# Two ways to turn and spread memory probabilities in a recurrent attention kernel, and where twenty tail units stand

## The chip, the core and the metric

The kernel runs on one core of a Trainium2 chip. A core has five engines that work side by side: TensorE (PE, with its weight loads as PEld), VectorE (DVE), ScalarE (ACT), GpSimd (POOL) and SyncE (SP, which here issues most DMAs). The metric is device time in microseconds of one execution; lower is better. Line numbers with an L are those of the kernel before, unless the text says that they are of the changed kernel.

## What is computed

A layer norm, an attention with a recurrent memory over 64 segments, a second layer norm, and a feed-forward layer with squared relu, with two residual sums:

```python
h = x + A(layernorm(x)); out = h + B(layernorm(h))
# A: S = 2048 rows of Dm = 640, H = 32 heads of Dh = 128, M = 8 memory rows, segments of 32 rows
mem = mem0
for s in range(n_seg):
    h = jnp.concatenate([mem, xs], axis=1)            # 8 memory rows, 32 rows of the segment
    q, k, v = (einsum('btd,dhe->bhte', h, W) for W in (Wq, Wk, Wv))
    p = softmax(where(mask, q @ k.T * Dh ** -0.5, -1e9))  # a memory row sees all, a row only earlier ones
    o = einsum('bhte,hed->btd', p @ v, Wo)
    mem = o[:, :M]; outs.append(o[:, M:])
```

The memory rows of one segment's output are input of the next. This makes a chain of 64 steps that cannot be done side by side.

## The kernel before

**Segments.** Each call of `step(b, sp)` (L462) is one segment, s = 4b + sp. Its projections run over 32 rows: the 8 memory rows, and the first 24 rows of the segment. The last 8 rows of each segment ("tails") have their projections made in advance, four segments to a block of 32 rows: 16 blocks, four to a group. A group's tail rows are loaded with `load_tail_rows` (L125), normalised (`ln_stats`, `ln_norm`), transposed (`ln_transpose`, L197) and kept in `hTt`. Groups 0 to 2 are transposed on PE at the start of the kernel; group 3 (blocks 12 to 15) is loaded by four DMAs in segment 3 and transposed by a DMA in segment 6.

**Fill.** The tail projections are cut into units of four matmuls of 512 columns (`tail_units`, L324), and the wo projection of a finished block's tails into ten units of four or eight matmuls (`wo_tail_units`, L368). A plan (L901 to L931) holds them with a due segment and a segment from which they can run; `portion(s)` takes some for each segment, up to 8.05 per segment on average and nine at most, none in segment 0. They go to `fill`, and `run(fill, n)` issues them in PE's stream between the segment's own work. Values of a block's tails go to DRAM (`vt_d`) and come back as `vt4`.

**One segment on PE**, in the order of its stream: q (L562 on), k, q, k projections of two halves of the heads; scores of the memory rows for the first half of the heads (`scores(0)`, L505); v projection in pieces; scores of the segment's rows (`token_scores`, L601); `scores(1)`; the rest of v; some fill; values of the memory rows for the first half (`values(0)`, L551 and L556); more fill; the first 16 matmuls of the output projection wo (L270); `values(1)`; the other 48 of wo; the rest of the fill; values of the rows of the segment before (`token_values`, L426 and L431). Then o is summed out of PSUM (`wo_out`, L285 to L287) and turned into the next segment's hT (`mem_to_hT`, L387), for which the next q projection waits.

**Memory softmax.** For each half n of the heads, `soft1(n)` takes the maximum on DVE (L511) and the exponential on ACT (L516). `soft2(n)` takes the reciprocal of the sum (L522) and writes the four copies of the tail probabilities (L523). The probabilities lie as 128 rows (four groups g of 32) by 64 columns. The values matmul wants them turned, 32 x 32 by 32 x 32, and spread over a tile `pB` of 128 x (4 x 64) that is zero outside block (g, g). The two halves do this in different ways:

- Half 0 scales to 64 columns (L527), turns them (L538, `soft3`), and copies the four blocks into a `pB[0]` that was zeroed at the start (L541): one block by ACT, two by POOL, one by DVE, the last behind the maximum of half 1 (`then` of `soft1`).
- Half 1 multiplies with `own` while it scales (L530, 256 columns; `own` is 1 for the row's own group and 0 elsewhere, read with a broadcast), and turns all 256 columns (L533).

**Segment 0** has its projections done beforehand, in `start()` (L813), while the weights arrive: wv, wq, wk and then wo in eight pieces, all on SP's queue. `stream("q", ...)` and `stream("k", ...)` (L837) issue five pieces of the main projection each, with units of blocks 3 to 9 between them; five units are left over for segment 0. `SEG0` (L764) says how many units stand ahead of each quarter of wo in segment 0: none.

Of the kernel before, what the change touches and what calls it, by code (L numbers as in the profile page):

```python
# [9 lines left out]
ALU = mybir.AluOpType  # L10
# [6 lines left out]
def kernel(  # L17
# [16 lines left out]
    nc = tc.nc  # L34
# [90 lines left out]
    def load_tail_rows(g, eng=nc.sync):  # L125

        xt = s2.tile([128, D], BF16, tag="xt", name="xt")
        if g > 2:
            for b in range(4):
                eng.dma_start(out=xt[32 * b:32 * b + 32, :],  # L130
                              in_=x2d.rearrange("(b s t) d -> b t s d", s=4, t=SEG)[4 * g + b, HD:SEG, :, :])
        else:
            eng.dma_start(out=xt[:], in_=x2d.rearrange("(s t) d -> s t d", t=SEG)[16 * g:16 * g + 16, HD:SEG, :])
        xts["t", g] = xt

    o_ring = [const.tile([128, DQ], BF16, name="o%d" % k) for k in range(5)]
# [60 lines left out]
    def ln_transpose(b):  # L197

        xn = xns.pop(b)
        if not isinstance(b, tuple) and b > 0:  # L200
            nc.sync.dma_start(out=rows_in(b), in_=xn[:], transpose=True)
            return
        if isinstance(b, tuple) and b[1] > 2:
            hTt = s2.tile([128, DC, 4, TL, 4], BF16, tag="hTt", name="hTt", bufs=4)
            nc.sync.dma_start(out=hTt[:].rearrange("p c b k s -> p c (b k s)"), in_=xn[:], transpose=True)
            hTts[b[1]] = hTt
            return
        pt = mm.tile([128, 1024], BF16, tag="mm", name="pt")
        for c in range(DC):
            nc.tensor.transpose(out=pt[:, c * 128:(c + 1) * 128], in_=xn[:, c * 128:(c + 1) * 128], identity=ident[:])  # L210

        def out():
            if isinstance(b, tuple):
                hTt = s2.tile([128, DC, 4, TL, 4], BF16, tag="hTt", name="hTt", bufs=4)
                for dve, a0, a1 in ((False, 0, 12), (True, 12, 20)):
                    evac(dve, hTt[:].rearrange("p c b k s -> p (c b) s k")[:, a0:a1],
                         pt[:, 0:640].rearrange("p (a s k) -> p a s k", s=4, k=TL)[:, a0:a1])
                hTts[b[1]] = hTt
                return
            ptv = pt[:, 0:640].rearrange("p (c s t) -> p c s t", c=DC, s=4)  # L220
            nc.scalar.copy(out=rows_in(b).rearrange("p c (s t) -> p c s t", s=4)[:, :, :, 0:HD], in_=ptv[:, :, :, 0:HD])
        return out
# [239 lines left out]
    def step(b, sp, v=None):  # L462
# [43 lines left out]
                                     start=(j == 0), stop=(j == 3), skip_group_check=True)  # L506
            sms[n] = sm

        def soft1(n, then=None):
            mx = s2.tile([128, 1], F32, tag="mx", name="mx")  # L510
            nc.vector.tensor_reduce(out=mx[:], in_=sms[n][:, 0:NK], op=ALU.max, axis=AX.X, negate=True)  # L511
            if then:
                then()
            em = s2.tile([128, SEG + NK], BF16, tag="em", name="em", bufs=1)
            zm = s2.tile([128, 1], F32, tag="zm", name="zm")
            nc.scalar.activation(out=em[:, SEG:], in_=sms[n][:, 0:NK], func=ACT.Exp, bias=mx[:, 0:1], scale=1.0,  # L516
                                 accum_out=zm[:])
            ems[n], zms[n] = em, zm

        def soft2(n):  # L520
            rm = s2.tile([128, 1], F32, tag="rm", name="rm")
            nc.vector.reciprocal(out=rm[:], in_=zms[n][:])  # L522
            nc.vector.tensor_tensor(out=ems[n][:, 0:SEG].rearrange("p (j k) -> p j k", k=TL),  # L523
                                    in0=ems[n][:, 2 * SEG:].unsqueeze(1).to_broadcast([128, 4, TL]), in1=same[:], op=ALU.mult)
            if n == 0:
                pm = s1.tile([128, HG, TL], BF16, tag="pkt", name="pm")[:].rearrange("p i k -> p (i k)")
                nc.vector.tensor_scalar(out=pm, in0=ems[n][:, 0:2 * SEG], scalar1=rm[:, 0:1], scalar2=None, op0=ALU.mult)  # L527
                return pm
            pm = s1.tile([128, HG, 32], BF16, tag="pk", name="pm")[:].rearrange("p (g a) k -> p g (a k)", g=G)
            nc.vector.scalar_tensor_tensor(out=pm, in0=ems[n][:, 0:2 * SEG].unsqueeze(1).to_broadcast([128, G, 2 * SEG]),  # L530
                                           scalar=rm[:, 0:1], in1=own[:].unsqueeze(2).to_broadcast([128, G, 2 * SEG]),
                                           op0=ALU.mult, op1=ALU.mult)
            nc.vector.transpose(out=pBs[1][:], in_=pm)  # L533
            return pBs[1]

        def soft3(pm):
            pT = s1.tile([128, 2, 32], BF16, tag="pTt", name="pT")[:].rearrange("p u k -> p (u k)")
            nc.vector.transpose(out=pT, in_=pm)  # L538
            def part(g):
                r = slice(32 * g, 32 * g + 32)  # L540
                (nc.vector.tensor_copy, nc.scalar.copy, nc.gpsimd.tensor_copy, nc.gpsimd.tensor_copy)[g](out=pBs[0][r, g], in_=pT[r])  # L541
            for g in range(1, G):
                part(g)
            return pBs[0], lambda: part(0)

        def values(n, pB, po):
            cols = po[:, 0, 0:128]
# [49 lines left out]
        def token_scores(n):  # L597
            skv = view()
            for j in range(4):
                for g in range(G):  # L600
                    nc.tensor.matmul(skv[32 * g:32 * g + 32, n * 4 + j, :], lhsT=qT[:, n * 16 + g * 4 + j, :],  # L601
                                     rhs=kT[:, n * 16 + g * 4 + j, :], start=True, stop=True,
                                     skip_group_check=True)

        token_scores(0)
        if not ready:
            proj(wv, "half", lhs, 0, ps0, 2, DC)
# [2 lines left out]
            proj(wv, "half", lhs, 1, ps1, 0, 1)  # L610
        if not last:
            pm0 = soft2(0)
            pT0, then = soft3(pm0)
            scores(1)
            soft1(1, then)
        if not ready:
            proj(wv, "half", lhs, 1, ps1, 1, 2)
        token_scores(1)
# [4 lines left out]
            if last:  # L623
                nc.scalar.copy(out=v[:, 768:1024], in_=ps1[:, 256:512])
        if not last:
            pT1 = soft2(1)
        def causal(skv):
            nc.vector.tensor_tensor(out=skv[:, :, M:NK], in0=skv[:, :, M:NK],
                                    in1=mask[:].unsqueeze(1).to_broadcast([128, HG, SEG]), op=ALU.add)

        held = []
        if ready:
            run(fill, 10)
            run_late(0, 100)
        skv = view()
        po = po_tiles()
        if last:
            run(fill, 2, held, True)
            token_values(s - 1, *prevs[-2], po)
            token_out(s - 1, po)  # L640
            settle(held, True)
            run(fill, 100, held)
            settle(held, True)
            causal(skv)
        else:
            ahead = 0 if ready else (len(fill) + 1) // 2
            left = len(fill) - ahead
            run(fill, (ahead - 1) // 2, held, True)
            values(0, pT0, po[1][0])
            values_out(0, po[1][0])  # L650
            if not ready:
                nc.scalar.copy(out=v[:, 768:1024], in_=ps1[:, 256:512])
            run(fill, len(fill) - left, held)
            pw = chn.tile([128, 512], F32, tag="ch", name="pw")
            if not ready:
                wo_rounds(lambda p: oT[:, p, M:NK], pw, range(4))
            values(1, pT1, po[1][1])
            causal(skv)
            values_out(1, po[1][1])
            settle(held, True)  # L660
# [23 lines left out]
        if not last:  # L684
            if ready:
                for k in range(4):
                    run(fill, SEG0[k])
                    wo_rounds(lambda p: oT[:, p, M:NK], pw, [2 * k + h for h in (0, 1, 8, 9)])
            else:
                wo_rounds(lambda p: oT[:, p, M:NK], pw, range(4, 16))  # L690
# [70 lines left out]
    parked += [(hnT0[:, c, :], True) for c in range(DC)] + [(ht0[k][:, 0:512], True) for k in range(NK4)]  # L761
    parked += [(t, True) for t, _ in halves(oTts[1][:].rearrange("p h r -> p (h r)"))]
    writes = []
    SEG0 = (0, 0, 0, 0)  # L764
    hnTs = [hnT0[:], ck(DC * NT).rearrange("p (c t) -> p c t", c=DC)]
    ots = [ck(D) for _ in range(4)]
    fxs = [ck(D) for _ in range(4)]
# [45 lines left out]
    def start():  # L813
# [45 lines left out]
        for n in range(2):  # L859
            spread(n)  # L860
        tails_v_in(0, nc.gpsimd, 0, 1)
        run(units, 10)
        parked.append((s1.tile([128, D], BF16, tag="xn", name="parkx")[:, 0:512], False))
        units += [u for b in (8, 9) for u in tail_units(b, "v")] + tail_units(1, "q")
        stream("k", wk, kT)
        units += tail_units(1, "k")
        run(units, DC)
        fill.extend(units)
# [10 lines left out]
    load_tail_rows(2)  # L879
    load_w(wv, A_Wv, 4, 5)  # L880
    load_w(wq, A_Wq)
    load_w(wk, A_Wk)
    load_wo()
    ln_transpose(("t", 0))()
    ln_stats(("t", 1))
# [5 lines left out]
    nc.gpsimd.memset(mask[0:TL], 0.0)  # L891
    nc.gpsimd.affine_select(out=mask[0:TL], in_=mask[0:TL], compare_op=ALU.is_ge, fill=NEG, base=HD,
                            pattern=[[-1, SEG]], channel_multiplier=1)
    nc.gpsimd.memset(pBs[0][:], 0.0)
    nc.gpsimd.memset(own[:], 0.0)
    for g in range(G):
        nc.gpsimd.memset(own[32 * g:32 * g + 32, g:g + 1], 1.0)
# [7 lines left out]
            plan += [(4 * b - 3 + (which == "k"), 4 * b - 5, u[DC * n:DC * n + DC]) for n in range(2)]  # L905
    for b in range(10, NB):
        u = tail_units(b, "v")
        plan += [(b - 8 if b < 12 else 28 + 4 * (2 * b - 24 + n), 1 if b < 12 else 7, u[DC * n:DC * n + DC]) for n in range(2)]
    for b in range(NB - 1):
        plan.append(({NB - 4: NS - 3, NB - 2: NS - 1}.get(b, min(4 * b + 8, NS - 3)), 4 * b + 5, wo_tail_units(b)))  # L910
    plan.sort(key=lambda p: p[0])
    begun, paced = [], [0]

    def portion(s):
        n = {NS - 3: 482, NS - 2: 486}.get(s, round(8.05 * s)) - paced[0]
        got = []
        while True:
            if not begun:
# [3 lines left out]
                plan.remove(ready[0])  # L922
                begun.append(ready[0])
            d, _, u = begun[0]
            if len(got) >= min(n, 9) and d > s:
                break
            got.append(u.pop(0))
            if not u:
# [4 lines left out]
    for b in range(NB):  # L933
        for sp in range(4):
# [16 lines left out]
                nook += ln_parts(b + 2)  # L951
            if 0 < b < NB - 1 and sp == 1:
                ln_transpose(b + 1)
            if (b, sp) == (0, 3):
                load_tail_rows(3)
            if (b, sp) == (1, 0):
                late.insert(0, (1.15, lambda: ln_stats(("t", 3)), 4))
            if (b, sp) == (1, 1):
                mid.append(lambda: ln_norm(("t", 3)))
            if (b, sp) == (1, 2):  # L960
                ln_transpose(("t", 3))
            e = b * 4 + sp - (NS - 7)
            if (b, sp) == (1, 0):
                ffn_biases()
# [138 lines left out]
```

## Time and profile before

| what | us |
|---|---|
| median of three runs | 946.59 |
| the three runs | 945.86, 946.59, 948.37 |
| the profiled execution | 946.84 |
| its span, first to last instruction | 945.0 |
| start to the first segment's scores | about 50 |
| segments 1 to 62, each | 11.74 to 13.90 |

The profiled execution's span is 1.8 us shorter than its time. The mean granted clock of TensorE is 0.998 of full speed. PE executes 24760 matmuls. A timeline line reads: start, length (both in us), engine, source line, operation, output <- inputs, shape, count; a bracket gives the idle time of that engine before it and what ended it. A line of the windows view reads: stretch, length, and then busy time and number of instructions of PE, PEld, DVE, ACT and POOL, granted clock, share of the DMA engines, and GB/s. A line of the chain view in order of time reads: start, length, what.

### The profile page before, as it was taken

The page shows a single profiled execution, that of the slowest core. Times are in us where ns is not written, and L with a number is a line of the kernel's source. Part 1 is how long each engine was busy: PE and PEld are TensorE (multiplying, and loading weights), DVE is VectorE, ACT ScalarE, POOL GpSimd, SP SyncE. Part 2 cuts the span into 40 slices and gives each one's busy share as a digit, 9 for nine tenths or more (in the row PEclk, how much of TensorE's full clock was granted, in tenths as well). Part 3 has the DMA queues.
Part 4 walks back from the last instruction along what each step waited for, and adds up shares of the span by engine and source line. Part 5 has one row for each costly group of instructions (what it writes and reads, how often), then busy time and mean ns, then how long its engine had stood idle before and what let it go on. Part 6 is the DMA issues. An engine that isn't in the chain of part 4 may idle for free.

```text
span 945.0 us, 56036 instructions
## 1 busy us (share of the span) xinstructions
PE 918.3 (97%) x24760; PEld 524.0 (55%) x24760; DVE 681.4 (72%) x2068; ACT 571.7 (60%) x1586; POOL 309.7 (33%) x1003
## 2 busy tenths in 40 slices
PE   5979999999999999999999999999999999999998
PEld 2435555655565555555555555565555555565555
DVE  5167887777777777877787787777777788556632
ACT  2446666666666666766676666666666666523321
POOL 2023333333333333333333333333333344344300
PEclk9999999999999999999999999999999999999999
DMA  9982201020102001110101010101010221733320
GB/s 359 408 263 67 45 14 34 9 35 9 22 20 26 19 15 25 20 21 14 32 17 29 9 32 15 32 12 33 15 32 13 53 44 22 233 82 91 91 56 28
DMA packets 65779, 56.66 MB, mean 60 GB/s; under 512 B 37288, under 2 KB 61616, under 8 KB 63616
## 3 DMA queue, kind: packets, MB, share of 16 engines
q1 hardware_dynamic: 65392, 52.74, 20.1%
q8 instruction: 194, 3.18, 1.4%
q14 instruction: 49, 0.40, 0.1%
q0 software_dynamic: 128, 0.33, 0.1%
q10 hardware_dynamic: 16, 0.01, 0.0%
HBM read 38.37 MB, written 9.44 MB: 51 GB/s over the span
## 4 chain that ended last, share of the span: by engine, by line
PE 91%; DMA 4%; SPq 2%; DVE 1%; issue 1%; ACT 1%; DVEq 0%
PE ps L234 23%; PE px L234 21%; PE pw L270 15%; PE pk L234 7%; PE y L1060 6%; PE ps L1008 6%; PE ps L270 3%; PE po L551 2%; DMA wq<-in_A_Wq_dram 2%; PE po L426 2%; SPq L151 2%; PE ps L601 1%; PE sm L505 1%; DMA wo<-in_A_Wo_dram 1%; DMA wv<-in_A_Wv_dram 1%; PE po L556 1%
## 5 line engine op out<-in xcount | busy, mean ns | idle before, releaser
L234 PEld LDWEIGHTS <-hT 128*32 128x32 bf16 x7680 | 180.4, 96 | 160.4 <-DVE hT L387 20.4
L270 PE MATMUL pw<-wo,oT 128*32 128x320 bf16 x4224 | 168.8, 299 | 2.5 <-DMA wo<-in_A_Wo_dram 2.3
L234 PE MATMUL px<-wv,hT 128*32 128x512 bf16 x2520 | 166.0, 377 | 0.0
L270 PEld LDWEIGHTS <-oT 128*32 128x32 bf16 x4224 | 107.7, 96 | 41.6 <-ACT oT L246 19.6
L258 DVE STREAM_TRANSPOSE qT<-row 128x512 bf16<-128x512 bf16 x128 | 89.2, 697 | 36.1 <-ACT row L253 36.0
L679 POOL TENSOR_TENSOR pkt<-ek,rk 128x64 bf16<-128x64 bf16 x64 | 19.0, 296 | 257.0 <-ACT otmp L286 255.4
L234 PE MATMUL ps<-wq,hT 128*32 128x512 bf16 x1260 | 82.7, 387 | 2.7 <-DVE hT L387 2.4
L234 PE MATMUL ps<-wk,hT 128*32 128x512 bf16 x1280 | 80.2, 379 | 0.0
L234 PE MATMUL px<-wq,hT 128*32 128x512 bf16 x1260 | 79.1, 379 | 0.0
L234 PE MATMUL pk<-wk,hT 128*32 128x512 bf16 x1240 | 78.2, 380 | 0.0
L1016 ACT ACTIVATE wv<-ps,b1f 128x512 bf16<-128x512 f32 (+1 forms) x56 | 37.6, 672 | 66.6 <-PE ps L1008 65.7
L437 ACT CAST oT<-po 128x512 bf16<-128x512 f32 x128 | 68.8, 589 | 11.6 <-PE po L431 6.6
L246 ACT CAST oT<-po 128x128 bf16<-128x128 f32 x126 | 33.6, 266 | 63.0 <-PE po L556 58.3
L234 PEld LDWEIGHTS <-hTt 128*32 128x32 bf16 x1920 | 50.7, 96 | 36.2 <-issue 1.7
L451 POOL COPY qz<-qT 128x96 bf16<-128x96 bf16 x126 | 33.6, 267 | 112.7 <-DVE qT L258 112.6
L1060 PE MATMUL y<-wq,wk 128*128 128x320 bf16 x416 | 58.9, 299 | 0.2
L492 ACT CAST row<-ps 128x256 bf16<-128x256 f32 x126 | 40.8, 375 | 29.9 <-PE ps L234 29.9
L253 ACT ACTIVATE row<-ps 128x512 bf16<-128x512 f32 x93 | 54.9, 610 | 6.3 <-PE ps L234 5.1
L253 ACT ACTIVATE row<-px 128x512 bf16<-128x512 f32 x63 | 37.6, 597 | 32.1 <-PE px L234 32.1
L285 ACT COPY otmp<-pw 64x96 f32<-64x96 f32 (+2 forms) x129 | 29.0, 225 | 45.5 <-PE pw L270 23.3
L287 DVE TENSOR_TENSOR o<-pw,otmp 128x96 bf16<-128x96 f32 (+2 forms) x129 | 31.4, 243 | 27.6 <-ACT otmp L286 21.4
L258 DVE STREAM_TRANSPOSE kT<-row 128x512 bf16<-128x512 bf16 x65 | 45.0, 692 | 7.9 <-ACT row L246 7.5
(141 smaller groups left out, 1840.0 us busy)
## 6 DMA issues: line engine op xcount, KB each, us to landing
wv<-in_A_Wv_dram SPq DMA_DIRECT2D x5, 1024.0 KB
wq<-in_A_Wq_dram SPq DMA_DIRECT2D x5, 1024.0 KB
wk<-in_A_Wk_dram SPq DMA_DIRECT2D x5, 1024.0 KB
wo<-in_A_Wo_dram SPq DMA_DIRECT2D x8, 640.0 KB
o_all<-o SPq DMA_DIRECT2D x256, 7.5 KB
vt<-vt_d SPq DMA_DIRECT2D x15, 256.0 KB
xt<-in_A_x_dram SPq DMA_DIRECT2D x19, 160.0 KB
wq<-in_B_w_dram SPq DMA_DIRECT2D x1, 2080.0 KB
```

The source lines that it names most:

```text
L234: nc.tensor.matmul(ps[32 * k:32 * k + 32, :], lhsT=lhs(c), rhs=wr[:, c, n, k], start=(c == 0), stop=(c == DC - 1))
L246: nc.scalar.copy(out=out_, in_=in_)
L253: nc.scalar.mul(out=row, in_=ps, mul=scale)
L258: nc.vector.transpose(out=dst[:, n * 16:(n + 1) * 16, 0:32], in_=row.rearrange("p (h e) -> p h e", e=32))
L270: nc.tensor.matmul(pw[32 * j:32 * j + 32, c0:c0 + DH], lhsT=lhs(p), rhs=wov2[:, head(p), ch], start=(h == 0), stop=(h == 15))
L287: nc.vector.tensor_tensor(out=five(o[:])[:, cs], in0=blocks(0, 128, 32)[:, cs], in1=five(tmp[:])[:, cs], op=ALU.add)
L437: nc.scalar.copy(out=oTg[:, gs, :, :, 0:SEG], in_=po[1][h][:, :, 0:256].rearrange("p g (n j q) -> p g n j q", n=2, q=32))
L451: nc.gpsimd.tensor_copy(out=d.rearrange("p a (j f) -> p a j f", j=3)[:, :, :, 0:M], in_=src[:, :, 0:3, :])
L492: nc.scalar.copy(out=row[:, u * 256:(u + 1) * 256], in_=ps[:, u * 256:(u + 1) * 256])
L1008: nc.tensor.matmul(ps[:], lhsT=w1[:, c, fc * 128:(fc + 1) * 128], rhs=hnT[:, c, :], start=(c == 0), stop=(c == DC - 1))
L1016: nc.scalar.activation(out=r[:, 0:w], in_=ps[:, 0:w], func=ACT.Relu, bias=b1f[:, fc:fc + 1], scale=1.0)
L1060: nc.tensor.matmul(y[hh][:, 0:DH], lhsT=f1T[:, fc, k * 128:(k + 1) * 128], rhs=w2[:, fc, cs], start=(fc == 0 and not hf), stop=(fc == FFUL ...
```

## The change

Half 0 and half 1 of the memory softmax now go the same way: scale to 64 columns, turn 64 columns, and one product with `own`, broadcast, into `pB`. The maximum of half 1 stands ahead of the turn of half 0 on DVE. The copies on ACT, POOL and DVE, the zeroing of `pB[0]`, the 256-column scale and the 256-column turn are gone.

```diff
-        def soft1(n, then=None):
+        def soft1(n):
...
             nc.vector.tensor_reduce(out=mx[:], in_=sms[n][:, 0:NK], op=ALU.max, axis=AX.X, negate=True)
-            if then:
-                then()
...
-            if n == 0:
-                pm = s1.tile([128, HG, TL], BF16, tag="pkt", name="pm")[:].rearrange("p i k -> p (i k)")
-                nc.vector.tensor_scalar(out=pm, in0=ems[n][:, 0:2 * SEG], scalar1=rm[:, 0:1], scalar2=None, op0=ALU.mult)
-                return pm
-            pm = s1.tile([128, HG, 32], BF16, tag="pk", name="pm")[:].rearrange("p (g a) k -> p g (a k)", g=G)
-            nc.vector.scalar_tensor_tensor(out=pm, in0=ems[n][:, 0:2 * SEG].unsqueeze(1).to_broadcast([128, G, 2 * SEG]),
-                                           scalar=rm[:, 0:1], in1=own[:].unsqueeze(2).to_broadcast([128, G, 2 * SEG]),
-                                           op0=ALU.mult, op1=ALU.mult)
-            nc.vector.transpose(out=pBs[1][:], in_=pm)
-            return pBs[1]
-
-        def soft3(pm):
+            pm = s1.tile([128, HG, TL], BF16, tag="pkt", name="pm")[:].rearrange("p i k -> p (i k)")
+            nc.vector.tensor_scalar(out=pm, in0=ems[n][:, 0:2 * SEG], scalar1=rm[:, 0:1], scalar2=None, op0=ALU.mult)
+            return pm
+
+        def soft3(n, pm):
             pT = s1.tile([128, 2, 32], BF16, tag="pTt", name="pT")[:].rearrange("p u k -> p (u k)")
             nc.vector.transpose(out=pT, in_=pm)
-            def part(g):
-                r = slice(32 * g, 32 * g + 32)
-                (nc.vector.tensor_copy, nc.scalar.copy, nc.gpsimd.tensor_copy, nc.gpsimd.tensor_copy)[g](out=pBs[0][r, g], in_=pT[r])
-            for g in range(1, G):
-                part(g)
-            return pBs[0], lambda: part(0)
+            nc.vector.tensor_tensor(out=pBs[n][:], in0=pT.unsqueeze(1).to_broadcast([128, G, 2 * SEG]),
+                                    in1=own[:].unsqueeze(2).to_broadcast([128, G, 2 * SEG]), op=ALU.mult)
+            return pBs[n]
...
             pm0 = soft2(0)
-            pT0, then = soft3(pm0)
             scores(1)
-            soft1(1, then)
+            soft1(1)
+            pT0 = soft3(0, pm0)
...
-            pT1 = soft2(1)
+            pT1 = soft3(1, soft2(1))
```

The 20 units of the tail values of blocks 10 and 11 move from segments 1 to 3 into segment 0, at places that `SEG0` now gives; the later segments get 7.717 units on average. Group 3 of the tails is loaded by one DMA among the weights, between the first and second piece of wk, and normalised and transposed on PE during `start()`, like groups 0 to 2; its values may run from segment 1 on. In every segment the units ahead of `values(0)` become fewer: with seven or eight units, none instead of one.

```diff
+        if ready:
+            run(fill, SEG0[0])
         token_scores(0)
...
         if ready:
-            run(fill, 10)
+            run(fill, SEG0[1])
             run_late(0, 100)
...
-            ahead = 0 if ready else (len(fill) + 1) // 2
+            ahead = SEG0[2] if ready else (len(fill) + 1) // 2
             left = len(fill) - ahead
-            run(fill, (ahead - 1) // 2, held, True)
+            run(fill, (ahead - 1) // 4, held, True)
             values(0, pT0, po[1][0])
...
-                    run(fill, SEG0[k])
+                    run(fill, SEG0[3 + k])
...
-    SEG0 = (0, 0, 0, 0)
+    SEG0 = (4, 5, 4, 0, 0, 5, 5)
...
         run(units, 10)
+        ln_stats(("t", 3))
+        ln_norm(("t", 3))
...
-        stream("k", wk, kT)
+        stream("k", wk, kT, lambda: ln_transpose(("t", 3))())
...
-    load_w(wk, A_Wk)
+    load_w(wk, A_Wk, 0, 1)
+    load_tail_rows(3)
+    load_w(wk, A_Wk, 1, DC)
...
-        plan += [(b - 8 if b < 12 else 28 + 4 * (2 * b - 24 + n), 1 if b < 12 else 7, u[DC * n:DC * n + DC]) for n in range(2)]
+        plan += [(0 if b < 12 else 28 + 4 * (2 * b - 24 + n), b // 12, u[DC * n:DC * n + DC]) for n in range(2)]
...
-        n = {NS - 3: 482, NS - 2: 486}.get(s, round(8.05 * s)) - paced[0]
+        n = {NS - 3: 482, NS - 2: 486}.get(s, round(20 + 7.717 * s)) - paced[0]
...
-            if len(got) >= min(n, 9) and d > s:
+            if len(got) >= min(n, 9 if s else 20) and d > s:
```

More of the change, by code (lines that the diff above doesn't have):

```diff
@@ L127, in load_tail_rows @@
         xt = s2.tile([128, D], BF16, tag="xt", name="xt")
[L128 to L133, printed above, removed]
+        eng.dma_start(out=xt[:], in_=x2d.rearrange("(s t) d -> s t d", t=SEG)[16 * g:16 * g + 16, HD:SEG, :])
         xts["t", g] = xt
@@ L201, in ln_transpose @@
             nc.sync.dma_start(out=rows_in(b), in_=xn[:], transpose=True)
[L202 to L206, printed above, removed]
             return
@@ L893 @@
                             pattern=[[-1, SEG]], channel_multiplier=1)
-    nc.gpsimd.memset(pBs[0][:], 0.0)
     nc.gpsimd.memset(own[:], 0.0)
@@ L953 @@
                 ln_transpose(b + 1)
[L954 to L961, printed above, removed]
             e = b * 4 + sp - (NS - 7)
```

## The prediction

> **What bounds the kernel now.** I read the page first (busy time, chain that ended last, costliest groups), then PE's waits, then the timeline of segment 0 and of one steady segment, then the start of every segment.
>
> ```profile
> PE 918.3 (97%) x24760; PEld 524.0 (55%) x24760; DVE 681.4 (72%) x2068; ACT 571.7 (60%) x1586; POOL 309.7 (33%) x1003
> ...
> PE 91%; DMA 4%; SPq 2%; DVE 1%; issue 1%; ACT 1%; DVEq 0%
> ```
>
> This says "TensorE, all the way": 97% busy, 91% of the chain. But matmuls are pipelined and their ends are modelled, so a busy PE can hide short waits. I therefore compared periods. Two full segments (20 and 21, eight fill units each) and two of the last (61 and 62, with two and four wo units of the tail):
>
> ```profile
> 289.72:301.50 11.78, 11.78 (x367) 6.59 (x360) 8.78 (x29) 8.38 (x25) 3.95 (x14) 1.00 0.07 18
> 301.50:313.28 11.78, 11.78 (x367) 6.58 (x360) 9.79 (x31) 8.36 (x25) 3.94 (x14) 1.00 0.43 57
> 779.04:790.82 11.78, 10.91 (x340) 6.03 (x341) 10.31 (x34) 8.07 (x25) 4.81 (x17) 1.00 0.11 24
> 790.82:802.60 11.78, 11.28 (x352) 6.26 (x352) 9.69 (x32) 7.48 (x23) 4.69 (x16) 1.00 0.10 21
> ```
>
> The period is 11.78 us in all four, though the later ones hold 1.3 and 0.9 us less of fill (a unit of four-column matmuls takes 0.216 us from start to start). So fill is free, and the recurrence from one segment's memory to the next sets the period. Its three joints are in the segment that starts at 433.00:
>
> ```profile
> 438.82 0.27 PE L505 MATMUL sm<-kT,qz 128*32 128x40 bf16 x16
> ...
> 438.88 0.24 DVE L527 TENSOR_SCALAR pm<-em,rm 128x64 bf16<-128x64 bf16 x1
> ...
> 439.23 0.24 DVE L538 STREAM_TRANSPOSE pT<-pm 128x64 bf16<-128x64 bf16 x1
> ...
> 439.40 0.16 DVE L511 TENSOR_REDUCE mx<-sm 128x1 f32<-128x40 f32 x1
> ...
> 439.60 0.51 POOL L541 COPY pB<-pT 32x64 bf16<-32x64 bf16 x2 [0.89 <-DVE mx L511]
> ...
> 440.17 0.28 PE L551 MATMUL po<-pB,v 128*32 128x32 bf16 x16
> ...
> 440.98 0.45 DVE L533 STREAM_TRANSPOSE pB<-pm 128x256 bf16<-128x256 bf16 x1
> ...
> 441.57 0.42 PE L551 MATMUL po<-pB,v 128*32 128x32 bf16 x16
> ```
>
> The first values matmul starts at 440.17, 0.05 us after POOL's second copy ends (440.11); that gap is the same in 60 of 63 segments. PE was free at 439.89; one fill unit (0.22) covers most of the wait. The second values matmul starts at 441.57, 0.15 after the transpose at L533 ends (441.43), again in nearly all segments. The third joint is the memory's turn into hT: the next q projection starts 0.05 after L387 in 47 of 62 segments, and wo's end to that start is 1.19.
>
> Segment 0 has another end:
>
> ```profile
> 49.44 10.12 DMA wo<-in_A_Wo_dram
> ...
> 59.60 0.73 PE pw L270 x14
> ...
> 61.50 2.33 PE ps L234 x20
> 63.82 1.38 PE pk L234 x19
> ```
>
> The last piece of wo lands at 59.56 and releases the chain. PE waits 6.7 us in all between 48.8 and 61.6, and afterwards it is slow: the windows show a granted clock of 0.95 up to 61.50 and 0.60 from there to 65.00; the first two projections take 2.11 and 1.42 us from start to start, where 1.08 is usual.
>
> **The change, part by part.**
>
> *Units moved to segment 0.* Of 20 units (blocks 10 and 11), 23 with the left-over ones stand in four waits of segment 0: 4 (0.86) before the first token scores (wait 1.1), 5 where five stood, 4 before the second values (wait 1.1), 5 and 5 (2.16) in the waits for wo (2.3). All fit, with some 0.3 us left before the last wo piece; beyond that cover each costs 0.22. Segments 1 to 59 get seven or eight units where eight or nine stood. By the equal periods that is worth nothing, except in segments 11, 30 and 50, which had nine and took 11.84, 12.03 and 12.00: about -0.5 together.
>
> *Clock.* With PE kept at work up to 61 us I expect no slow stretch: 2.11 + 1.42 - 2 x 1.08 = **-1.37**. Bounds: -1.37 and 0.
>
> *Tail group 3 early.* Five transposes on PE, 0.38 from start to start as at 22.22; statistics, scaling and evacuation (0.89, 0.21, 0.40, 0.74 on DVE, 1.03 on ACT) stand where DVE is busy 2.7 of 12 us and ACT 5.6. Both lie ahead of the wo wait, which hides them. Its load is not hidden: 160 KB are queued on SP ahead of four pieces of wk and all of wo. wk lands some 3 us before its use, wo does not; at the 362 to 419 GB/s of these stretches it lands **+0.4** later. Four more writes of tail values (some 1 us each on SP's queue, after wo's issue ends at 51.1) delay the loads behind them (vt for step 1, x for blocks 1 and 2), which are needed from 69.8 on. The four loads and the DMA transpose that leave segments 3 to 6 waited for nobody there: nothing.
>
> *First half.* On DVE: the max of the second scores now comes ahead of the turn, and the turn is followed by one 128x256 multiply in place of copies on DVE, ACT, POOL and POOL. Rules from the rows: a DVE instruction that depends on nothing new starts 0.08 before its predecessor's end, a dependent one 0.035 after; DVE follows a matmul's end by 0.04 to 0.07 (L1044). So: second scores end 439.09, max 439.14 to 439.30, turn 439.22 to 439.47, multiply from 439.50. Its length is not in the trace. Below: 0.28, the plain bf16 product of this width at L1017. Above: 0.485, L530, which multiplies by the same broadcast `own`, with a scalar besides. Nearest: the sum at L628, 256 wide with a broadcast operand, 0.40. L1017 at 256 and L786 at 640 (0.28, 0.48) give a fixed 0.145 and, at half their rate, 0.27 for 256 columns: I take **0.41**. The multiply ends 439.92.
>
> The row speaks first: 0.28 for two plain operands against 0.485 with `own`. [...]
>
> What the end releases: in the built program, the weight load of the first values now carries the wait for DVE, as that of the second does today, where the matmul comes 0.145 later; today's first one holds the wait for POOL in the matmul and comes 0.05 later. So the first values start at 440.06 instead of 440.17. But no unit stands ahead of them any more: PE idles 0.17, and the unit is now between the values. From there PE has 0.157 (values) + 4 x 0.216 + 0.547 (16 matmuls of wo) and reaches the second values at 441.63, against 441.57: **+0.056**. Cover on the way: oT from ACT at about 440.75, before wo asks for it.
>
> *Second half.* Exp follows the earlier max at 439.42 (after ACT's v copy) instead of 439.77; then reciprocal 439.84, product with `same`, scaling 0.24, turn 0.245, multiply 0.41: pB ready at 441.08, matmul possible at 441.22. Before: 441.57. This gain of 0.35 is not on the path, since PE arrives at 441.63. It shows only where few units stand: segments 60, 61, 62, together -0.6.
>
> Behind the second values (wo, o, hT) nothing changes; with three units instead of four there PE only waits longer for hT.
>
> **Sum**, against the profiled execution (946.84; span 945.0, 1.8 around it): 0.4 - 1.37 - 0.5 - 0.6 + 55 x 0.056 (= 3.1) = +1.0, so 947.8. The median of the runs, 946.59, lies 0.25 below that execution: **947.6**.
>
> **Rivals.**
> 1. *The multiply runs at 0.28.* First values 439.93, second 441.50: -0.07 in 55 segments instead of +0.056, 7 us less: **940.6**. For: L1017. [...] Chance 0.17.
> 2. *Slower: the wait for the first probabilities stretches.* The max now holds DVE until PE's second scores are seen, with turn and multiply queued behind. The first scores end at 437.59 and their max starts at 437.79; DVE was busy until then, so up to 0.20 instead of 0.05 is possible, and the multiply may take L530's 0.485. Each 0.1 us costs 5.8. It decides against the kernel from first values at 440.09 on (0.03 later than I expect); with 0.485 it gives **951.8**, with the full 0.20 **956**. Chance 0.25.
> 3. *PE is the bound after all, and the 20 units are worth their 4.3 us:* **943.3**. For: 97% and the chain. Against: the four equal periods. Chance 0.05.
> 4. *The fill does not do its work* (clock drops anyway, or wo waits for units): +1.4, **949**. Chance 0.08.
>
> **Numbers.** Forecast 947.6, chance 0.45, its own range 944.5 to 950.5 (multiply by 0.03 either way: 1.7; PE's unexplained "issue" waits, 4 us in total, will fall elsewhere). 0.3% is 2.8 us, about what a measurement of this kernel can tell from no change. Faster: rival 1, rival 3 and a little of the forecast, 0.22. Slower: rival 2 and 0.07 of forecast and rival 4, 0.32. Same: 0.46. The range goes from rival 1 to beyond rival 2's first price: 940 to 953.
>
> **What would show it.** The multiply (L520 of the changed kernel) at 0.41; first values 0.145 after its end and 0.17 after PE was free; a steady period of 11.83 or 11.84; segments 60 to 62 shorter than 11.78; q of segment 1 at 61.9 with a granted clock of 1.0 after it. I am wrong if the period falls below 11.78 (the multiply is fast) or exceeds 11.87 (the max waits), or if the period follows the number of units.

## The result, and the profile after

The changed kernel takes **953.12 us** (median of six runs, 950.34 to 956.22) where the kernel before took 946.88 (six runs, 945.86 to 948.37): ratio **1.0058, interval 1.0043 to 1.0073**. It is slower, by 0.6%, clear of the noise. The profiled execution took 952.4 us with a span of 950.5, against 945.0. From here on line numbers are those of the changed kernel, unless a fence is of another.

The page of the changed kernel, busy time and the chain by engine:

```profile
PE 921.3 (97%) x24765; PEld 532.3 (56%) x24765; DVE 696.5 (73%) x2132; ACT 557.1 (59%) x1524; POOL 279.4 (29%) x876
...
PE 85%; DVE 10%; ACT 2%; issue 2%; POOL 0%; DMA 0%; ACTq 0%; DVEq 0%
```

PE is as "busy" as before; but DVE holds 10% of the chain where it held 1%. The last chain now goes through DVE in most segments. Two full segments (28, 29) and the last two (61, 62) in the windows view:

```profile
388.45:400.37 11.92, 11.84 (x362) 6.70 (x362) 9.03 (x30) 7.67 (x23) 3.47 (x12) 1.00 0.04 10
400.37:412.27 11.90, 11.82 (x367) 6.68 (x360) 9.99 (x32) 8.05 (x24) 3.46 (x12) 1.00 0.23 58
784.48:796.08 11.60, 10.77 (x341) 6.08 (x341) 10.54 (x35) 7.85 (x24) 4.34 (x15) 1.00 0.12 25
796.08:808.10 12.02, 11.40 (x352) 6.62 (x353) 9.89 (x33) 7.28 (x22) 4.20 (x14) 1.00 0.11 21
```

The period of full segments is **11.91** instead of 11.78, with seven units and with eight. The joint, in the timeline of segment 36:

```profile
490.82 0.24 DVE L514 TENSOR_SCALAR pm<-em,rm 128x64 bf16<-128x64 bf16 x1
...
491.12 0.20 DVE L501 TENSOR_REDUCE mx<-sm 128x1 f32<-128x40 f32 x1
...
491.24 0.23 DVE L519 STREAM_TRANSPOSE pT<-pm 128x64 bf16<-128x64 bf16 x1
...
491.51 0.43 DVE L520 TENSOR_TENSOR pB<-pT,own 128x256 bf16<-128x256 bf16 x1
...
492.08 0.28 PE L529 MATMUL po<-pB,v 128*32 128x32 bf16 x16
...
492.24 1.05 PE L224 MATMUL ps<-wq,hTt 128*32 128x512 bf16 x16
...
492.67 0.42 DVE L520 TENSOR_TENSOR pB<-pT,own 128x256 bf16<-128x256 bf16 x1
...
493.10 0.73 PE L260 MATMUL pw<-wo,oT 128*32 128x320 bf16 x16
493.64 0.28 PE L529 MATMUL po<-pB,v 128*32 128x32 bf16 x16
```

PE was free at 491.83 and starts the first values at 492.08, 0.25 later; then four units and 16 matmuls of wo, and only then the second values, 1.81 after it was free (1.69 before). Their `pB` had been ready since 493.09; with 0.15 from there to the first matmul they could have started 0.40 earlier.

Segment 0, in the chain view in order of time:

```profile
55.74 0.72 PE pw L260 x14
56.47 2.49 issue
58.95 0.58 PE pw L260 x10
59.53 1.08 PE ps L224 x20
60.61 0.54 PE pw L260 x16
61.16 1.08 PE ps L224 x20
62.23 0.56 PE pw L260 x16
```

PE stops for 2.49 us within wo's second quarter, and the profile names no releaser. The last of wo's eight pieces landed at 61.24 (59.56 before); the last quarter of wo starts only at 61.94, since the stop, ten units and the third quarter stand ahead of it. Segment 1 starts at 63.96 (61.50 before) and its q and k run at a granted clock of 1.00 (windows view, 63.96 to 67.00).

The 5.5 us of span divide so: 0.3 before PE's 300th recorded instruction (19.19 and 19.49; over the 13 profiles of this study 19.19 to 21.18, so chance); 0.5 from there to PE's first wait in segment 0; 1.7 from that wait to segment 1; -1.0 in segment 1; +3.8 in segments 2 to 59; +0.3 in 60 to 62; nothing behind (rounded parts).

### The profile page after: what moved, and what is told of

Read it like the earlier page. It is cut to its first block, busy times and chain, and to the rows that moved or that the text cites. A ratio compares the mean times of both kernels' runs of the same rounds, so it can differ in the third digit from the quotient of the medians.

```text
span 950.5 us, 55841 instructions
## 1 busy us (share of the span) xinstructions
PE 921.3 (97%) x24765; PEld 532.3 (56%) x24765; DVE 696.5 (73%) x2132; ACT 557.1 (59%) x1524; POOL 279.4 (29%) x876
## 4 chain that ended last, share of the span: by engine, by line
PE 85%; DVE 10%; ACT 2%; issue 2%; POOL 0%; DMA 0%; ACTq 0%; DVEq 0%
PE ps L224 25%; PE pw L260 15%; PE px L224 14%; PE pk L224 7%; PE y L1035 6%; PE ps L983 6%; PE ps L260 3%; DVE pB L520 3%; PE po L529 2%; DVE pT L519 2%; PE po L416 1%; PE sm L495 1%; PE pa L224 1%; DVE kT L485 1%; PE po L534 1%
## 5 line engine op out<-in xcount | busy, mean ns | idle before, releaser
L224 PEld LDWEIGHTS <-hT 128*32 128x32 bf16 x7680 | 183.3, 96 | 159.8 <-DVE hT L377 26.3
L260 PEld LDWEIGHTS <-oT 128*32 128x32 bf16 x4224 | 110.1, 96 | 42.5 <-ACT oT L236 10.4
L520 DVE TENSOR_TENSOR pB<-pT,own 128x256 bf16<-128x256 bf16 x126 | 53.6, 426 | 4.3
```

The source lines that it names most:

```text
L224: nc.tensor.matmul(ps[32 * k:32 * k + 32, :], lhsT=lhs(c), rhs=wr[:, c, n, k], start=(c == 0), stop=(c == DC - 1))
L260: nc.tensor.matmul(pw[32 * j:32 * j + 32, c0:c0 + DH], lhsT=lhs(p), rhs=wov2[:, head(p), ch], start=(h == 0), stop=(h == 15))
L520: nc.vector.tensor_tensor(out=pBs[n][:], in0=pT.unsqueeze(1).to_broadcast([128, G, 2 * SEG]), in1=own[:].unsqueeze(2).to_broadcast([128, G ...
```

## Experiments

**Which half of the softmax change, and where the units stand.** Theory A: the period is set by the later of two ways to the second values; by way of the first values it holds the wait for the multiply *plus* all units behind them. The rival: the second maximum in the way of the first half is the loss, wherever units stand.

`e4_unit_ahead`: one number.

```diff
-            run(fill, (ahead - 1) // 4, held, True)
+            run(fill, (ahead - 1) // 2, held, True)
```

> The changed kernel with one number changed: one unit ahead of the first values again, three instead of four between the two. Theory A (the place of the unit): the stall of 0.25 ahead of the first values falls to 0.03, they start at the same time, and the second values come 0.21 earlier: period 11.70, time 953 - 56 x 0.21 = 941. Theory B (maximum, turn and multiply on DVE set the period through the second half): period stays 11.91, time 953. Theory C (the fill delays the first values): 12.1.

Measured: 944.42, ratio to before 0.9984 (0.9969 to 0.9998); period 11.695. PE's rows in segment 32 of this kernel:

```profile
437.26 0.39 PE L224 MATMUL ps<-wq,hTt 128*32 128x512 bf16 x4
437.51 0.28 PE L529 MATMUL po<-pB,v 128*32 128x32 bf16 x16
437.62 0.24 PE L534 MATMUL po<-pB,vt 128*32 128x128 bf16 x4
437.67 0.83 PE L224 MATMUL ps<-wq,hTt 128*32 128x512 bf16 x12
438.32 0.73 PE L260 MATMUL pw<-wo,oT 128*32 128x320 bf16 x16
438.86 0.28 PE L529 MATMUL po<-pB,v 128*32 128x32 bf16 x16
```

The first values start 0.25 after PE was free, as in the changed kernel, but a unit lies in that time; the second come 1.60 after. That is theory A's place, to the hundredth. The time fell by 7.0 by the two ratios, 8.7 by the medians, not by 12: more of that below.

`e1_softmax_only`: the kernel before, with the softmax diff alone.

> The kernel before with the softmax part of the change alone: units, plan, group 3 and the unit ahead of the first values stay as they were. Theory A (the place of the unit): the multiply releases the first values 0.25 after PE is free in any case; the unit that stands ahead of them fits into these 0.25, and three units instead of four stand between the two values, so the second values come at 0.25 + 0.16 + 3 x 0.216 + 0.55 = 1.60 after PE is free, against 1.69 before and 1.81 after: period 11.70 in segments of eight units, time 942 (0.08 less in some 55 segments). Theory B (the maximum ahead of the turn is the loss, wherever the units stand): period 11.9, time 953. Segment 1 starts at 61.5 as before.

Measured: 943.31, ratio 0.9971 (0.9954 to 0.9988), period 11.69 (11.83 and 11.91 in the two segments of nine units). So the softmax part by itself makes the kernel faster; in the profiles segments 2 to 59 take 687.9 us, against 691.9 before. Segment 1 started at 62.39, in line with a start that was 1.3 later in this execution.

`e3_turn_first`: turn and multiply ahead of the second maximum.

```diff
+            pT0 = soft3(0, pm0)
             scores(1)
             soft1(1)
-            pT0 = soft3(0, pm0)
```

> The changed kernel with the turn and the multiply of the first half ahead of the second maximum on DVE (in the order of before). By the rows of the changed kernel the turn then starts at once behind the scaling, 0.19 earlier, and the first values 0.06 after PE is free instead of 0.25: PE alone would reach the second values 0.19 earlier. But the second maximum waits until the multiply is over (0.47 later), and with it exponential, reciprocal, scaling, turn and multiply of the second half, whose values could start 0.11 later than now. Theory A (the later of the two chains sets the period): second values 0.11 later, period 12.02, time 953 + 57 x 0.11 = 959. Theory B (the maximum in the first half's way is the whole loss): period 11.72, time 942.

Measured: 968.0, ratio 1.0209 (1.0192 to 1.0227), period 12.16. The side is theory A's, the size is not: the second values came 0.25 later, not 0.11. DVE in this kernel:

```profile
500.93 0.24 DVE L514 TENSOR_SCALAR pm<-em,rm 128x64 bf16<-128x64 bf16 x1
501.28 0.25 DVE L519 STREAM_TRANSPOSE pT<-pm 128x64 bf16<-128x64 bf16 x1
501.56 0.42 DVE L520 TENSOR_TENSOR pB<-pT,own 128x256 bf16<-128x256 bf16 x1
501.90 0.19 DVE L501 TENSOR_REDUCE mx<-sm 128x1 f32<-128x40 f32 x1
```

The turn does not start at once behind the scaling but 0.11 after its end (as in the kernel before: 439.12 and 439.23). So the maximum ahead of it costs the first half only 0.06 (wait 0.19 instead of 0.25), and taking it away delays the second half by far more. Its place ahead is right.

`e5_own_wide`: `own` as 16 equal columns for each group, so that both operands have step 1 along 16 columns.

```diff
-    own = const.tile([128, G], BF16)
+    own = const.tile([128, G, 16], BF16)
...
-            nc.vector.tensor_tensor(out=pBs[n][:], in0=pT.unsqueeze(1).to_broadcast([128, G, 2 * SEG]),
-                                    in1=own[:].unsqueeze(2).to_broadcast([128, G, 2 * SEG]), op=ALU.mult)
+            nc.vector.tensor_tensor(out=pBs[n][:].rearrange("p g (a b) -> p g a b", b=16),
+                                    in0=pT.rearrange("p (a b) -> p a b", b=16).unsqueeze(1).to_broadcast([128, G, 4, 16]),
+                                    in1=own[:].unsqueeze(2).to_broadcast([128, G, 4, 16]), op=ALU.mult)
```

> The changed kernel with own kept as 16 equal columns for each group, so that the multiply reads both operands with step 1 along 16 columns. If the step of 0 is what makes the multiply slow, it takes about 0.28 (the plain product of that width) instead of 0.426: first values 0.145 earlier, period 11.77, time 953 - 57 x 0.145 = 945. If the outer broadcast or the width decides, it stays at 0.43: period 11.91, time 953. That the slower rival of the prediction holds (the time from the maximum to the first values sets the period one for one) shows in the ratio of the two differences: 1 if true, 0 if not.

Measured: 946.14, ratio 0.9994 (0.9979 to 1.001), period 11.78. The group in the costliest-groups view of this kernel (count, busy us, mean ns, idle before):

```profile
L520 DVE TENSOR_TENSOR pB<-pT,own 128x256 bf16<-128x256 bf16 x126 | 36.9, 293 | 4.3
```

293 ns instead of 426: 0.133 less, and 0.13 of period for it. This wait ahead of the first values was paid in full.

**Segment 0.** `e2_fill_only`: the changed kernel with the softmax of before and one unit ahead again.

> The changed kernel with the softmax of before and the old number of units ahead of the first values; the units in segment 0, the plan and group 3 stay changed. Period 11.78 as before in all theories. Theory A (the 20 units in segment 0 make PE stop, by themselves or by the instructions they add while wo loads): PE stops by some 2.5 us in wo's quarters again, segment 1 starts near 64 and is 1.0 shorter: time 946.6 + 2.5 - 1.0 - 0.5 = 947.5. Theory B (the stop falls on a place in the instruction stream by chance, or belongs to the softmax change): it is gone, segment 1 starts at 61.5 to 61.9, time 945.

Measured: 948.71, ratio 1.0026 (1.0012 to 1.0039); period 11.77; PE stops again, 2.56 us from start to start (2.78 in the changed kernel, counted in the same way), segment 1 at 64.11. The stop belongs to the fill, not to the softmax.

What is it? The DMA view of the changed kernel from 55 to 63 us has a queue of instructions:

```profile
q1 hardware_dynamic: 3362, 2.64, 101.7%
q8 instruction: 2, 0.03, 1.6%
```

Over the whole run this queue moves 194 packets of 16 KB; PE has 49757 recorded instructions (24765 weight loads, as many matmuls, 227 others), about 256 for each packet. I numbered PE's recorded instructions and listed its gaps over 0.24 us (from start to start) that end 1.2 to 1.75 us after such a packet has landed: in the profile before 15 of 21, in the changed one 15 of 29 lie at exactly the same place, **193 modulo 256**, and no other place holds more than two; the 2.49 is among them (after instruction 1729). The gaps at this place add up to 7.8 us before and 9.2 after.

`e6_shift60`: 60 more PE instructions long before.

```diff
-        for c in range(DC):
+        for c in list(range(DC)) * (7 if b == ("t", 0) else 1):
             nc.tensor.transpose(out=pt[:, c * 128:(c + 1) * 128], in_=xn[:, c * 128:(c + 1) * 128], identity=ident[:])
```

> The changed kernel with 60 more PE instructions early on: the five transposes of the first tail group stand seven times instead of once, writing the same values, long before segment 0. Theory A (PE's stop of 2.5 us in segment 0 and the scattered stops without a cause later are PE out of instructions: each stop lies at a multiple of 256 of PE's recorded instructions, plus 193, and ends 1.2 to 1.6 after the end of a 16 KB transfer of the instruction queue): the stop in segment 0 comes again ahead of recorded instruction 1730, which is now 60 instructions earlier in the program, ahead of or at the start of wo's first quarter instead of after 22 of its matmuls, and the later stops stay at 193 modulo 256. Theory B (a wait for a semaphore of wo's pieces that the profile does not show): the stop stays after 22 of wo's matmuls. Time within 2 us of 953 in both.

Measured: 954.62, ratio 1.0065 (1.005 to 1.0081). The stop came after recorded instruction 1729 again, now in the middle of the second values, ahead of wo (chain view of this kernel):

```profile
57.38 0.12 PE po L529 x12
57.50 2.37 issue
59.88 0.20 PE po L529 x4
...
60.51 1.00 PE pw L260 x24
61.51 1.08 PE ps L224 x20
```

14 of the 23 gaps listed in the same way lie at 193 modulo 256 (14 of 20 with the narrower limit of 1.6 that I had expected). The wait goes with the count of instructions and not with the place in the program: theory A.

`e8_placed_early` and `e7_placed`. The first moves segment 0's units ahead of wo, on top of the second, which places the units of the other segments.

```diff
-            ahead = SEG0[2] if ready else (len(fill) + 1) // 2
+            ahead = SEG0[2] if ready else max(len(fill) - 4, 0)
...
-            run(fill, (ahead - 1) // 4, held, True)
+            run(fill, max(ahead - 1, 0) // 2, held, True)
...
-    SEG0 = (4, 5, 4, 0, 0, 5, 5)
+    SEG0 = (6, 8, 9, 0, 0, 0, 0)
```

> The changed kernel with own as 16 columns for each group, and all units but four ahead of the second values, half of them less one ahead of the first (one ahead and two or three between). Theory A (PE's own work up to the second values is now the bound, both chains being ahead of it): period 11.66 with eight units (0.03 of stall less than with one unit ahead alone) and 11.45 with seven, so that the period follows the number of units; 944.4 - 58 x 0.03 - 45 x 0.28 x 0.216 to 58 x 0.28 x 0.216 = 939 to 940. Theory B (a chain that the profile does not show keeps the period): 11.66 to 11.70 in both, time 943.

> The kernel of the run beside it with the 23 units of segment 0 all ahead of the output projection (6, 8, 9, 0, 0, 0, 0 instead of 4, 5, 4, 0, 0, 5, 5). Theory A (PE is out of instructions for 2.5 us after recorded instruction 1729, whatever stands there, and work left behind the stop is pushed past the landing of wo): the stop comes at the same instruction, ahead of wo's first quarter or in it, and the ten units that stood behind it no longer do: segment 1 starts 1.5 to 2 us earlier, at 62 to 62.5; time 1.5 to 2 less than the run beside it. Theory B (the stop is of wo's second quarter): segment 1 stays at 64.

`e7_placed`: 940.77, ratio 0.993 (0.9908 to 0.9951). Its windows, a segment of eight units and one of seven:

```profile
429.18:440.84 11.66, 11.66 (x368) 6.62 (x362) 8.85 (x30) 7.59 (x23) 3.49 (x12) 1.00 0.04 10
583.23:594.80 11.57, 11.57 (x365) 6.51 (x358) 9.84 (x32) 7.69 (x23) 3.48 (x12) 1.00 0.31 57
```

With eight units PE is the bound (no wait before either values); with seven, only two units stand between the values, and wo waits 0.13 for oT, ACT's copy of the first values (wo starts 0.05 after ACT's end in all nine such segments); so 11.57 and not the 11.45 I had expected.

`e8_placed_early`: 939.35, ratio 0.9904 (0.9879 to 0.993). The stop came after instruction 1729 once more, only 0.8 long since PE got there later: the moved units now meet a wait of 1.24 for DVE ahead of it. From PE's first wait in segment 0 to segment 1 it took 13.34 us against 14.36 in `e7_placed`: 1.0 saved, where 1.5 to 2 was expected, and segment 1 started at 63.88, not at 62 to 62.5. The intervals of the two ratios overlap, so the times do not tell them apart.

`e9_no_group3`: the changed kernel with the fourth tail group as before.

> The changed kernel with the fourth tail group as before (loaded in segment 3, transposed by a DMA in segment 6); softmax, units in segment 0 and the number ahead of the first values stay changed. In the runs so far the stretch from PE's 300th recorded instruction to its first wait in segment 0 is 30.12 us in all kernels with the early group and 29.62 in the two without. Theory A (the early group itself costs 0.5 ahead of segment 0): 29.62 here, segment 1 0.5 earlier against the same point, time 952.5. Theory B (the 0.5 belongs to the 20 units or to the order of the work around them): 30.12, time 953.

Measured: 952.07, ratio 1.006 (1.0043 to 1.0078). The stretch took 29.61: the early group costs 0.5 ahead of segment 0. PE stopped after instruction 1729 again (2.70 from start to start), so the stop does not need the early group. The times do not tell 0.5, and a slow stretch of the clock lay in the rest of this profile (granted clock 0.67 from 60 to 64 us).

**The clock.** `e10_before_again`, one run of the kernel before, 949.2.

> The kernel before, unchanged, for a second profile. Theory A (the slow stretch of the clock comes once at a moment of its own, whatever PE does): it lies elsewhere than between 61 and 65 us, or is missing; segment 1 then takes about 11.75 instead of 13.90. Theory B (PE's waits for wo bring it, as the prediction had it): again 0.6 between 61.5 and 65, segment 1 at 13.9.

Theory A falls. The windows of this second profile of before:

```profile
56.00:61.00 5.00, 2.35 (x50) 1.27 (x54) 2.26 (x5) 0.47 (x1) 0.00 (x0) 1.00 1.08 346
61.00:68.00 7.00, 5.83 (x62) 2.11 (x58) 2.40 (x8) 1.89 (x6) 2.32 (x8) 0.51 0.72 218
```

Half the clock at the same place, for twice as long, and segment 1 takes 14.84.

**A version that beats both.** `e11_placed_old_fill`: softmax, wide `own` and placing of `e7_placed` on the fill of before.

> The softmax change with own as 16 columns and all units but four ahead of the second values, on the fill of before (no units moved to segment 0, fourth group late). Theory A (the softmax part with the units well placed is the gain, the 20 units in segment 0 cost more than they bring): segment 1 starts 2 to 2.3 earlier than with the new fill against the same point, the period is 11.66 in segments of eight units and 11.87 in the two of nine, mean 0.01 to 0.03 above that of the same placing with the new fill: time about 940.8 - 2.2 + 1 = 939.6. Theory B (fewer units for each segment are worth more): 943 or more.

Measured: **939.27**, ratio 0.9928 (0.9913 to 0.9944). Against PE's 300th instruction segment 1 started 2.7 earlier than in `e7_placed` (0.5 of it the early group); the period is 11.65, and 11.83 and 11.86 in the two segments of nine units. As fast as `e7_placed` and `e8_placed_early` without moving any unit.

## Where the prediction held and where it failed, by its own steps

On the prediction's scale the changed kernel stands at 952.1 (1.0058 times 946.59): inside the range of 940 to 953, close to its upper edge, and 4.5 above the forecast of 947.6. Slower was the right way, but +1.0 was forecast and +5.5 came by the ratio, +6.2 by the medians. The range held because it was stretched towards the second rival, not because the sum was right: three steps failed (the chain of the first half, the fill of segment 0 and the landing of wo), and two terms came out near by luck.

**The mechanism held.** The recurrence, not the number of units, sets the period (11.91 with seven and eight units); the weight load that carries the wait brings the first values 0.145 after the multiply; PE alone sets the second values from there; the second half's gain of 0.35 is hidden; hT is followed by q as before.

**"Multiply from 439.50 ... ends 439.92" was too early by 0.08.** Against the moment when PE was free, the maximum starts 0.04 later than I put it and lasts 0.20, where the same maximum took 0.16 behind the turn; the turn follows 0.01 sooner than I put it, and the multiply takes 0.426 instead of 0.41. So PE waits 0.25, not 0.17, and the period grows by 0.13 and not 0.056: the edge that I had named (over 11.87, "the max waits"). My 0.41 was an estimate, from L1017 and L786 of the kernel before at half their rate; no run varies the width of this product, so the rate itself is not shown. At its one width the runs show 426 ns with `own` as one column for each group, and 293 ns in `e5_own_wide`, where the inner step of `own` is 1 instead of 0 and an outer step of 0 stays. These 133 ns are what half the rate would add, an estimate from the same two rows (0.20 us more for 384 columns more, so 0.133 for 256).

**"55 segments x 0.056 = 3.1" became 3.8**, though 58 x 0.13 is 7.5: that the term came out near is luck. Segments 2 to 59 lie on average 0.15 above their clean period before and 0.08 after. Where PE waits 0.19 or more ahead of the first values in most segments (after, `e3`, `e6`, `e9`), this excess is 0.07 to 0.11; where it waits 0.12 or less (before twice, `e1`, `e2`, `e4`, `e5`, `e7`, `e8`, `e11`), 0.13 to 0.17. Most of it lies where PE stops for instructions: before, the 13 of these 58 segments that hold a gap over 0.24 at 193 modulo 256 have 6.7 of the 8.7 us of excess, after, 11 segments have 4.5 of the 4.9. The stops seem to be paid partly out of a wait that is there anyhow, which fits that `e4` regained less than 12; no run shows this by itself. The prediction's "unexplained 'issue' waits, 4 us in total" are these stops: the idle time at this place in the profile before is 3.9.

**"All fit, with some 0.3 us left": failed.** The units were counted in PE time; that a packet of instructions landed during the waits of segment 0 (at 56.70 in the kernel before, where PE reached instruction 1729 at 59.75) was not counted. In the changed kernel PE was there at 56.17, and the packet landed at 57.61. From PE's first wait to segment 1 it took 1.7 of the 5.5 more, a term that I had at zero. PE had no long wait left behind the stop: segment 1 started 5.01 after its end in the changed kernel and in `e2`, `e3`, `e4` and `e7` alike.

**"Lands +0.4 later": too small.** The last piece of wo landed at 61.24 instead of 59.56, 1.7 later. Over all profiles it landed at 60.84 to 61.91 with the early group and at 59.56 to 60.77 without it, 1.1 later on average, so part of the 1.7 is chance. The early group also delays PE's own start by 0.5. In the profiles of the kernel before, `e1` and `e11` segment 1 started 1.93 to 1.94 after this landing, which released the last matmuls of wo. An estimate from these numbers is that without the stop segment 1 would have started at 63.2 and not at 61.50, so that of the 2.5 us to 63.96 the stop alone adds some 0.8. No run has the early group without the units, so this split is not shown.

**Clock -1.37: right in this profile, by luck**, -1.34 in the front of segment 1. The reason given, PE kept at work up to 61 us, did not hold: PE stopped for 2.49. With the units in segment 0, `e5_own_wide` and `e9_no_group3` did have half the clock for 3.41 us. The timed runs say the same. A mean granted clock of 0.998 fits one such stretch, and every run on record of the kernel before with a clock shows 0.998 or 0.996; of the six runs of the changed kernel three show 1.000 and three 0.998. So the gain came in about half of the runs. The segment as a whole gained 1.02, since a stop for instructions in it was 1.09 long, against 0.73 before.

**Segments 11, 30 and 50, -0.5: two of three.** 11 and 50 took 11.90 and 11.91, the usual period; 30 took 12.31, with a stop for instructions in it.

**Segments 60 to 62, -0.6: right only where no stop falls in.** +0.3 in this profile, since 60 and 62 each hold one; 11.60 each in `e6_shift60`.

**Rivals.** The second one was closest: it put the loss at the first values, with 5.8 us for each 0.1 (`e5_own_wide` gained 6.1 by the ratios for 0.133, 4.6 for each 0.1). It had a late maximum and a multiply of L530's length as its two causes; here the maximum ended 0.08 later than I put it, and the multiply was 0.016 over my value. The first fell with the multiply at 0.426, the third with the equal periods. The fourth saw the fill fail and priced it at 1.4 through the clock or through wo waiting for units; it was PE's stop for instructions and the work behind it, with a later wo beside it, and 1.7.

What stays open: why the packet that follows the 1473rd instruction is late (below) is inferred from its timing; no run took the wo load away. How the loss in segment 0 divides between the stop and the later wo is an estimate. And the split of the timed 6.2 us rests on single profiles.

## What to carry to other kernels

When a wait moves ahead of work, take the filler with it: here a unit in front of the wait was free, and the same unit behind it cost 0.21 of the period (11.91 against 11.70 in `e4_unit_ahead`). Shorten the chain ahead of an idle wait by making the broadcast operand contiguous along the inner axis, where a run shows that it pays (426 ns against 293 here). And count instructions, not only time, before filling waits during a weight load: PE, kept busy, reached its 1729th instruction at 56.17 instead of 59.75 here and stopped for 2.49. When a load is put ahead of others in a full queue, look up when the last of them lands (wo's last piece 1.1 later here, on average over the profiles).

## What the runs showed of the hardware

- **The instruction queue moved 194 packets of 16 KB while PE ran 49757 recorded instructions in the changed kernel (49751 in the kernel before), about 256 for each packet.** That the packets hold PE's instructions is inferred from these counts and from where PE stops. The packet after instruction 193 + 256k starts a median of 0.86 us after PE has passed there (0.80 to 1.00 over the profiles) and takes 1.0 to 1.1; where PE stops for over 0.24 us at such a place, it goes on some 1.4 after a packet has landed (a median of 1.39 before, 1.38 after). While the weights load (a DMA share of 1.01 to 1.07 between 10 and 56 us in the changed kernel) the packets come later: the first five 2.1 to 2.6 us after that point in the changed kernel, and the one of segment 0 3.65 to 4.00 us after in all profiles (3.87 in the changed kernel: 52.62 to 56.49). It came at nearly the same time after PE's 300th instruction (36.4 to 36.6 without the early group, 36.9 to 37.5 with it). In the changed kernel it landed at 57.61, PE had reached instruction 1729 at 56.17, and went on at 58.95, 1.34 after the landing. In the kernel before it landed at 56.70, PE reached instruction 1729 only at 59.75, and did not stop.
- **The granted clock was 0.5 for 3.41 us or twice that** (60.89 to 64.30 in the kernel before), in 6 of 13 profiles between 52 and 68 us: in all four with the waits of the old fill, in two of the nine with units in them (in `e11_placed_old_fill` it came twice, apart). Six of the eight profiles with a stop of 2.2 to 2.9 us there have no such stretch. Of the 56 runs on record of kernels with units in segment 0, 24 show a mean granted clock of 1.000 and 32 show 0.998.
- A DVE turn that reads the result just written started 0.11 after the scaling's end in the first half (`e3_turn_first` and the kernel before) and 0.03 in the second half of the changed kernel (492.36 and 492.39).
